# Where the streamed weight rows of a token-mixing kernel lie in SBUF

## The chip, the cores and the metric

The kernel runs on one core of one Trainium2 chip. The metric is device time in microseconds (us) of that core, as the median of several executions. TensorE (PE) does the matrix products, VectorE (DVE), ScalarE (ACT) and GpSimd (POOL) prepare operands and drain results, and SyncE (SP) issues the transfers.

SBUF, the memory from which all engines read, has 128 partitions. A tile occupies the same stretch of bytes in each partition. In this document a "word" is 4 bytes of one partition, and the "word of 64" of a row is its start address in words, modulo 64: a row that starts at byte 118,496 starts at word 29,624 and so at word 56 of 64.

## The reference

```
x  = causal 7-tap filter of x per head (softmax of `weight` as taps)     # 4 x 4224 x 192
theta = x @ w_theta
y  = w_tok_r @ (x * cos(theta)) + w_tok_i @ (x * sin(theta))             # w_tok: 4224 x 4224, twice
u  = x + y
x  = u + relu(u @ w_ch)
h  = U, V applied over the token axis (rank 32);  u = x + h
out = u + relu(u @ w_ch1) @ w_ch2                                         # 192 -> 768 -> 192
```

The two products with the 4224 x 4224 matrices `w_tok_r` and `w_tok_i` are most of the work. The weights arrive in 64-bit floating point. The kernel turns them into 32-bit values and splits each into an upper part (rounded for the matrix unit, type fp32r) and a lower part, the remainder.

## The kernel before

**Tokens and chunks.** The 4224 source tokens are 33 blocks of 128. The 4224 target tokens are nine chunks, `WIDE`: one of 480 columns, six of 464, two of 480. A step of `STEPS` is one chunk for two source blocks (a few steps at the start are two chunks for one block). For the last two source blocks the targets are eleven chunks of 384 (`LATE`).

**One group of matmuls.** `products` (L671) computes one output tile of 128 features by one chunk. For each of the two matrices (`q`) and each of the two source blocks (`k`) it issues three matmuls, L683: features' upper part by weights' upper row, upper by lower row, lower by upper row. That is 12 matmuls for a group, six groups for a step. The features (tile `z`) are the operand that is loaded into the array, 128 columns of it by a LDWEIGHTS ahead of each matmul. The weight row (tile `w`) is the operand that streams through. `evict` (L686) then adds the 128 x 464 or 128 x 480 sums into `yt` on DVE (L691).

**Where the rows lie.** The tile `w` (two buffers, pool `wp`, `weight_tile` at L607) has 8 x 480 words for each partition. `weight_part` (L595) cuts it: for the nine wide chunks the order is q, k, half, column, so an upper and a lower row of the same q and k stand 480 words apart, and 480 is 32 modulo 64. Half 0 is the lower row and half 1 the upper one. The eleven late chunks use another cut: all upper rows in the first half of the tile, all lower ones in the second, every row 448 words (7 x 64) after the last, from word 8 of the half on. The same tile serves after that for `w_ch1`, whose columns are then the loaded operand.

With the pools as they stand, both buffers of `w` begin at word 56 of 64. In the wide chunks lower rows are thus at word 56 and upper ones at word 24; late rows are all at word 0. The feature tiles `z` (pool `zp`, on the right-hand side) have all their blocks at word 24. Behind `wp` on the left lies `wraw`, the landing place of the raw weights. When it is given up, the tiles `hid`, `ot`, `vs` and `vt` of the last stage take its place, `hid` at word 40.

**The last stage.** For 22 pairs of batch and chunk, `up_mm` (L1158 to L1169) multiplies by `w_ch1` (five matmuls of 384 columns; the rows of `fq` at word 24 stream, blocks of `w` at word 8 are loaded) and `down` (L1200 to L1204) by `w_ch2` (five of 384; the rows of `hid` at word 40 stream, blocks of `cl` at word 24 are loaded).

**What sets the order.** The instruction order is written out by hand in tables (`OPENING`, `ENTRY`, `TURN`) and in between by the loop `mix`. While PE multiplies, ACT and DVE unpack and split the next weights (`split_w`), and the SP queue fetches the ones after that. None of the tables is touched.

Of the kernel before, what the change touches and what calls it, by code (L numbers as in the profile page):

```python
# [10 lines left out]
F32 = mybir.dt.float32  # L11
# [7 lines left out]
P = 128  # L19
# [12 lines left out]
COLS = 384  # L32
SPC = COLS // P
WIDTHS = [480] + [464] * 6 + [480] * 2
WIDE = [(sum(WIDTHS[:c]), w) for c, w in enumerate(WIDTHS)]
# [4 lines left out]
def mix_steps():  # L40

    def pairs(chunks, s):
        return [(s, 1, list(chunks[n : n + 2])) for n in range(0, len(chunks), 2)]

    steps = [(0, 1, [WIDE[0]])] + pairs(WIDE[1:EARLY], 0) + [(0, 2, [c]) for c in WIDE[EARLY:]]
    starts = [0, len(steps)]
    steps += [(1, 2, [c]) for c in WIDE[:EARLY]] + pairs(WIDE[EARLY:], 2)
    for s in range(3, NS, 2):  # L50
        starts.append(len(steps))
        steps += [(s, 2, [c]) for c in (WIDE if s < NS - 2 else LATE)]
    return steps, starts


EARLY = 5
STEPS, STARTS = mix_steps()


# [29 lines left out]
WSTEP = 480  # L89

LSTEP = 448
# [107 lines left out]
def mix_kernel(ctx, tc, xT, wcv, wth, wtok, wch, uu, vv, w1, w2, outT):  # L199
# [3 lines left out]
    def pool(name, bufs=1, side=None, space=None, stack=None):  # L203
        kw = dict(name=name, bufs=bufs, reuse_waits="tile")
        if side:
            kw["side"] = side
        if space is not None:
            kw["space"] = space
        return (stack or ctx).enter_context(tc.tile_pool(**kw))
# [52 lines left out]
    left = ExitStack()  # L262
# [2 lines left out]

    cst = pool("cst")
    yp = pool("yp")
    wp = pool("wp", bufs=2, stack=left)
    wrp = pool("wraw", bufs=2, stack=raw_st)

# [9 lines left out]
    with tc.manual_schedule():  # L280
# [314 lines left out]
        def weight_part(g, q, low):  # L595
            if g < n_chunks - len(LATE):
                kb, n, _ = pieces[2 * g]
                t = wt[g].rearrange("p (q k h n) -> p q k h n", q=2, k=2, h=2)
                return t[:, q, :kb, 1 - low, :n]
            t = wt[g][:, 4 * WSTEP * low : 4 * WSTEP * (low + 1)]  # L600
            if g < n_chunks:
                kb, n, _ = pieces[2 * g]
                t = t[:, 8 : 8 + 4 * LSTEP].rearrange("p (q k n) -> p q k n", q=2, k=2)
                return t[:, q, :kb, :n]
            return t[:, 2 * WSTEP * q + 16 : 2 * WSTEP * q + 16 + 2 * COLS]

        def weight_tile(g):  # L607
            if g not in wt:
# [2 lines left out]
        def split_w(g, q, part, eng=None):  # L611

            h = 2 * g + q
            if h >= len(pieces):
                return
            if part < 2:
                (unpack_parts, unpack_join)[part](raw[h])
                return
            if g > n_chunks:
                return  # L620
            weight_tile(g)
            hi, src = weight_part(g, q, 0), words(raw[h], 1, F32)
            if g < n_chunks:
                src = src.rearrange("p (k n) -> p k n", k=pieces[h][0])
            if part == 2:
                nc.scalar.copy(hi, src)  # L626
            else:
                eng = eng or (nc.gpsimd if g < STARTS[1] and h != 2 * OPENED + 3 else nc.vector)
                eng.tensor_tensor(out=weight_part(g, q, 1), in0=src, in1=f(hi), op=ALU.subtract)  # L629
                del raw[h]  # L630
                if h not in (2, 3):
                    load_w(h + 4 if h < 2 else h + 2)
# [38 lines left out]
        def products(g, j, r, q):  # L671
            s0, kb, ranges = STEPS[g]
            if q == 0:
                sums[g, j, r] = ps_mm.tile([P, WMAX], F32, name="acc", tag="acc")[:, : ranges[r][1]]
            ps = sums[g, j, r]
            n, last = q * kb * 3, kb * 6 - 1
            high, low = weight_part(g, q, 0), weight_part(g, q, 1)
            for i in range(kb):
                z = zt[s0 + i]
                zh = z[:, q, j * P : (j + 1) * P]  # L680
                zl = z[:, 2 + q, j * P : (j + 1) * P]
                for a, b in ((zh, high), (zh, low), (zl, high)):
                    mm(ps, a, b[:, i + r, :], start=n == 0, stop=n == last)  # L683
                    n += 1
# [409 lines left out]
        g = STARTS[-1]  # L1094
# [321 lines left out]
```

## Time and profile before

| | |
|---|---|
| median of 3 runs | 2964.04 us (2963.32 to 2964.55) |
| the profiled execution | 2963.67 us |
| its span, first to last instruction | 2961.9 us |
| PE busy in the span | 2948.1 us |
| DVE, ACT, POOL busy | 2495.3, 1554.3, 291.8 us |
| mean granted TensorE clock | 1.00 |
| matmuls at L683: of 464, 480 and 384 columns | 6696, 3348 and 792 |

A page of the profile gives busy times of the engines, a chain of work followed back from the last instruction, and groups of equal instructions. Matmuls overlap in the records (the duration of one is longer than the distance from its start to the next one's start), so what a matmul costs is read from starts: so many matmuls in so many microseconds of the chain, which lists PE's time without overlap.

### The profile page before, as it was taken

The page shows a single profiled execution, that of the slowest core. Times are in us where ns is not written, and L with a number is a line of the kernel's source. Part 1 is how long each engine was busy: PE and PEld are TensorE (multiplying, and loading weights), DVE is VectorE, ACT ScalarE, POOL GpSimd, SP SyncE. Part 2 cuts the span into 40 slices and gives each one's busy share as a digit, 9 for nine tenths or more (in the row PEclk, how much of TensorE's full clock was granted, in tenths as well). Part 3 has the DMA queues.
Part 4 walks back from the last instruction along what each step waited for, and adds up shares of the span by engine and source line. Part 5 has one row for each costly group of instructions (what it writes and reads, how often), then busy time and mean ns, then how long its engine had stood idle before and what let it go on. Part 6 is the DMA issues. An engine that isn't in the chain of part 4 may idle for free.

```text
span 2961.9 us, 39012 instructions
## 1 busy us (share of the span) xinstructions
PE 2948.1 (100%) x14994; PEld 2693.9 (91%) x14994; DVE 2495.3 (84%) x4133; ACT 1554.3 (52%) x2237; POOL 291.8 (10%) x254
## 2 busy tenths in 40 slices
PE   9999999999999999999999999999999999999999
PEld 8888888888888989898989898988889999999999
DVE  8799989888888888898989898989899897555555
ACT  7655545455555555554555554545456555444443
POOL 2110000010000000000000010100002002000000
PEclk9999999999999999999999999999999999999999
DMA  4443443443434434434334344343433221101110
GB/s 137 132 132 123 127 133 124 127 132 122 137 123 128 133 124 130 130 123 135 124 125 135 123 128 131 124 135 127 125 127 116 65 62 52 38 31 43 35 38 33
DMA packets 119002, 323.50 MB, mean 109 GB/s; under 512 B 6688, under 2 KB 40480, under 8 KB 118688
## 3 DMA queue, kind: packets, MB, share of 16 engines
q1 hardware_dynamic: 118416, 320.81, 33.6%
q8 instruction: 118, 1.93, 0.3%
q14 instruction: 68, 0.56, 0.1%
q10 hardware_dynamic: 400, 0.21, 0.0%
HBM read 308.01 MB, written 12.98 MB: 108 GB/s over the span
## 4 chain that ended last, share of the span: by engine, by line
PE 95%; DVE 4%; ACT 1%; issue 0%; DMA 0%; POOL 0%; DVEq 0%; POOLq 0%
PE acc L683 73%; PE ob L1201 2%; PE acc L1165 2%; PE acc L1169 2%; PE acc L1166 2%; PE oa L1202 2%; PE ob L1200 2%; PE oa L1204 2%; PE oa L1203 2%; PE acc L1167 2%; PE acc L1168 2%; PE pacc L912 1%; PE th L515 1%; PE th L516 1%; DVE yt L691 1%; PE th L518 1%
## 5 line engine op out<-in xcount | busy, mean ns | idle before, releaser
L683 PE MATMUL acc<-w,z 128*128 128x464 f32 (+2 forms) x10836 | 2287.3, 371 | 2.6 <-DVE yt L691 0.8
L683 PEld LDWEIGHTS acc<-w,z 128*128 128x128 f32 x10836 | 2018.7, 188 | 240.6 <-DVE yt L691 1.7
L691 DVE TENSOR_TENSOR yt<-acc,yt 128x464 f32<-128x464 f32 (+2 forms) x876 | 550.3, 634 | 213.3 <-PE acc L683 210.7
L626 ACT CAST w<-wraw 128x928 fp32r<-128x928 f32 (+3 forms) x291 | 303.5, 1043 | 635.1 <-DVE wraw L243 634.9
L238 DVE TENSOR_SCALAR wraw<-wraw 128x928 uint16<-128x928 uint16 (+4 forms) x305 | 368.8, 1210 | 11.8 <-ACT wraw L229 6.3
L629 DVE TENSOR_TENSOR w<-wraw,w 128x928 fp32r<-128x928 f32 (+2 forms) x282 | 365.0, 1294 | 0.0
L224 ACT ACTIVATE wraw<-wraw,consts 128x928 int32<-128x928 uint16 (+4 forms) x305 | 348.8, 1144 | 20.5 <-DMA wraw<-in_wtok 15.8
L243 DVE SCALAR_TENSOR_TENSOR wraw<-wraw 128x928 int32<-128x928 int32 (+4 forms) x305 | 342.0, 1121 | 10.1
L229 ACT ACTIVATE wraw<-wraw 128x928 f32<-128x928 f32 (+3 forms) x296 | 310.2, 1048 | 3.7 <-DMA wraw<-in_wtok 2.9
L577 POOL TENSOR_TENSOR z<-tz,z 128x384 fp32r<-128x384 f32 x121 | 125.2, 1034 | 1706.3 <-ACT z L574 1706.3
L452 DVE SCALAR_TENSOR_TENSOR xa<-xr,tap,xa 128x256 f32<-128x256 f32 x744 | 285.6, 425 | 0.0
L1177 DVE SCALAR_TENSOR_TENSOR hid<-acc,hid 128x384 fp32r<-128x384 f32 x264 | 146.9, 557 | 149.3 <-ACT hid L1174 148.3
L1174 ACT ACTIVATE hid<-acc 128x384 fp32r<-128x384 f32 x264 | 129.8, 492 | 250.2 <-PE acc L1169 233.8
L574 ACT CAST z<-tz 128x384 fp32r<-128x384 f32 x129 | 66.2, 513 | 289.4 <-DVE tz L563 289.3
L583 POOL TENSOR_TENSOR yt<-yt,xa 128x384 f32<-128x384 f32 x64 | 70.2, 1097 | 248.6 <-DVE xa L452 195.4
L1201 PE MATMUL ob<-hid,cl 128*128 128x384 f32 x264 | 89.2, 338 | 0.1
L1165 PE MATMUL acc<-fq,w 128*128 128x384 f32 x264 | 89.2, 338 | 0.0
L1169 PE MATMUL acc<-fq,w 128*128 128x384 f32 x264 | 89.0, 337 | 0.0
L1202 PE MATMUL oa<-hid,cl 128*128 128x384 f32 x264 | 88.8, 336 | 0.0
L1204 PE MATMUL oa<-hid,cl 128*128 128x384 f32 x264 | 88.8, 336 | 0.0
L1203 PE MATMUL oa<-hid,cl 128*128 128x384 f32 x264 | 88.8, 336 | 0.0
L1200 PE MATMUL ob<-hid,cl 128*128 128x384 f32 x264 | 88.7, 336 | 0.0
(239 smaller groups left out, 2655.2 us busy)
## 6 DMA issues: line engine op xcount, KB each, us to landing
wraw<-in_wtok SPq DMA_DIRECT2D x184, 928.0 KB, 4.7
wraw<-in_wtok SPq DMA_DIRECT2D x92, 960.0 KB, 4.9
wraw<-in_wtok SPq DMA_DIRECT2D x22, 768.0 KB, 4.4
xr<-in_xT SPq DMA_DIRECT2D x63, 201.0 KB, 2.6
outT<-ot SPq DMA_DIRECT2D x20, 576.0 KB, 3.0
vzw<-in_vv SPq DMA_DIRECT2D x10, 384.0 KB, 4.1
wraw<-in_w SPq DMA_DIRECT2D x3, 768.0 KB, 4.3
yt<-in_wtok SPq DMA_DIRECT2D x2, 928.0 KB, 8.8
```

The costliest lines, as they stand in the source:

```text
L224: nc.scalar.activation(words(raw, 0), words(raw, 1, U16), AF.Identity, scale=2.0**-13, bias=consts[:, 3:4])
L229: nc.scalar.activation(w, w, AF.Copy, scale=2.0**-112)
L238: nc.vector.tensor_scalar(out=words(raw, 1, U16), in0=words(raw, 3, U16), scalar1=0x8000, scalar2=None, op0=ALU.bitwise_and)
L243: nc.vector.scalar_tensor_tensor(out=words(raw, 1), in0=words(raw, 1), scalar=3, in1=words(raw, 0), op0=ALU.logical_shift_left, op1=ALU.bi ...
L452: nc.vector.scalar_tensor_tensor(out=xa, in0=src, scalar=w, in1=xa, op0=ALU.mult, op1=ALU.add)
L626: nc.scalar.copy(hi, src)
L629: eng.tensor_tensor(out=weight_part(g, q, 1), in0=src, in1=f(hi), op=ALU.subtract)
L683: mm(ps, a, b[:, i + r, :], start=n == 0, stop=n == last)
L691: nc.vector.tensor_tensor(out=dst, in0=ps, in1=dst, op=ALU.add)
L1165: mm(ps, w[0], q[:, b, :], start=True, stop=False)
L1169: mm(ps, w[3], q[:, 4 + b, :], start=False, stop=True)
L1201: mm(ob, c2[:, m, 2, :], h[:, 1, :], start=False, stop=last)
```

## The change

Three things are altered, none of which adds, removes or moves an instruction: each engine's list is the same as before, operation by operation and with the same waits.

- A pool `gap` of 16 words is allocated ahead of `wp`. All that lies behind it on the left moves by 16 words: `w` begins at word 8 of 64, `wraw` too, `hid` moves from word 40 to 56, and `ot`, `vs`, `vt` likewise.
- A table `ROWS` gives each wide chunk a pair (turn, skip). `turn` exchanges the places of the upper and the lower row, `skip` starts both rows 0, 8 or 16 words later inside their 480 words.
- The constants for the late chunks and for `w_ch1` are adjusted: late rows come to word 40 (from 0), `w_ch1` stays at word 8.

Upper / lower row, word of 64:

| chunk | columns | before | after |
|---|---|---|---|
| 0, 7 | 480 | 24 / 56 | 40 / 8 |
| 8 | 480 | 24 / 56 | 8 / 40 |
| 1 | 464 | 24 / 56 | 40 / 8 |
| 2 | 464 | 24 / 56 | 48 / 16 |
| 3 | 464 | 24 / 56 | 56 / 24 |
| 4 | 464 | 24 / 56 | 8 / 40 |
| 5 | 464 | 24 / 56 | 16 / 48 |
| 6 | 464 | 24 / 56 | 24 / 56 |
| late | 384 | 0 / 0 | 40 / 40 |

The features `z` stay at word 24.

```diff
@@
 EARLY = 5
+ROWS = {
+    o: r
+    for (o, _), r in zip(WIDE, [(0, 0), (0, 0), (0, 8), (0, 16), (1, 0), (1, 8), (1, 16), (0, 0), (1, 0)], strict=True)
+}
@@
     yp = pool("yp")
+    pool("gap", stack=left).tile([P, 16], F32, name="gap")
     wp = pool("wp", bufs=2, stack=left)
@@
                 t = wt[g].rearrange("p (q k h n) -> p q k h n", q=2, k=2, h=2)
-                return t[:, q, :kb, 1 - low, :n]
+                _, _, ((o, _), *_) = STEPS[g]
+                turn, skip = ROWS[o]
+                return t[:, q, :kb, 1 - low ^ turn, skip : skip + n]
             t = wt[g][:, 4 * WSTEP * low : 4 * WSTEP * (low + 1)]
             if g < n_chunks:
                 kb, n, _ = pieces[2 * g]
-                t = t[:, 8 : 8 + 4 * LSTEP].rearrange("p (q k n) -> p q k n", q=2, k=2)
+                t = t[:, 32 : 32 + 4 * LSTEP].rearrange("p (q k n) -> p q k n", q=2, k=2)
                 return t[:, q, :kb, :n]
-            return t[:, 2 * WSTEP * q + 16 : 2 * WSTEP * q + 16 + 2 * COLS]
+            return t[:, 2 * WSTEP * q : 2 * WSTEP * q + 2 * COLS]
```

## Rows read from the trace of the kernel before

**Rows 1.** The page, busy time of each engine, share of the span, instructions
```profile
span 2961.9 us, 39012 instructions
...
PE 2948.1 (100%) x14994; PEld 2693.9 (91%) x14994; DVE 2495.3 (84%) x4133; ACT 1554.3 (52%) x2237; POOL 291.8 (10%) x254
...
PEclk9999999999999999999999999999999999999999
```

**Rows 2.** The page, the chain that ended last, by engine and by line
```profile
PE 95%; DVE 4%; ACT 1%; issue 0%; DMA 0%; POOL 0%; DVEq 0%; POOLq 0%
```

**Rows 3.** Groups by shape: count, busy us, mean ns of one, idle before
```profile
L683 PE MATMUL acc<-w,z 128*128 128x464 f32 x6696 | 1411.5, 371 | 0.9 <-DVE yt L691 0.8
L683 PE MATMUL acc<-w,z 128*128 128x480 f32 x3348 | 731.7, 379 | 1.0 <-POOL z L577 0.7 <-ACT z L574 0.2
...
L683 PE MATMUL acc<-w,z 128*128 128x384 f32 x792 | 149.8, 340 | 0.7 <-DVE yt L880 0.7
```

**Rows 4.** Who waited for whom: us in total, times, longest
```profile
DVE yt L691 <- PE acc L683: 210.7, 229, 2.7
...
ACT wraw L224 <- DMA wraw<-in_wtok: 15.8, 25, 1.9
```

**Rows 5.** The chain, wide chunks, 1200 to 1420 us: start, us, what
```profile
1208.79 46.73 PE acc L683 x216
...
1256.77 30.11 PE acc L683 x144
...
1288.13 30.11 PE acc L683 x144
...
1319.49 30.20 PE acc L683 x144
...
1350.93 46.73 PE acc L683 x216
```

**Rows 6.** The chain, late chunks of 384 columns, 2290 to 2430 us
```profile
2297.15 9.38 PE acc L683 x54
2310.01 2.12 PE acc L683 x12
2313.13 2.09 PE acc L683 x12
...
2421.37 2.12 PE acc L683 x12
```

**Rows 7.** PE's instructions in order, last stage: start, us, line, shape
```profile
2563.78 0.34 PE L1200 MATMUL ob<-hid,cl 128*128 128x384 f32 x1
...
2564.65 0.34 PE L1165 MATMUL acc<-fq,w 128*128 128x384 f32 x1
...
2565.51 0.34 PE L1200 MATMUL ob<-hid,cl 128*128 128x384 f32 x1
```

**Rows 8.** DMA issues: size of each, median us from issue to landing
```profile
wraw<-in_wtok SPq DMA_DIRECT2D x184, 928.0 KB, 4.7
```

## The prediction

> **What bounds the kernel now.** I read the engines' busy times first. PE is busy for 2948.1 of 2961.9 us and the granted clock is in its top tenth in all forty slices, which is the 2.4 GHz level throughout [rows 1]. The chain that ended last says the same in another way: 95% of it is PE [rows 2]. The groups by shape say what on PE: L683 has 6696 matmuls of 464 columns, 3348 of 480 and 792 of 384, and PE stood idle ahead of the whole of them for 0.9, 1.0 and 0.7 us [rows 3]. So nothing that feeds or drains these matmuls is late. DVE waits 210.7 us in all for L683's sums [rows 4], which means that DVE is ahead of PE, and a raw weight tile lands 4.7 us after its issue [rows 8] while ACT waits for such transfers for 15.8 us in all [rows 4]. The time of this kernel is therefore a number of matmuls times the distance from the start of one to the start of the next, and only a change of that distance can change it much.
>
> **The distances.** In the chain, 216 matmuls of 480 columns take 46.73 us, 216.3 ns each, and 144 of 464 take 30.11 us, 209.1 ns each; one stretch of 144 takes 30.20 [rows 5]. As a yardstick I take one column for each cycle of 2.4 GHz: 200.0 and 193.3 ns. What is above that, the excess, is 16.3 ns for a 480 row and 15.8 ns for a 464 row. In the last stage ten matmuls of 384 columns, five of L1200 to L1204 and five of L1165 to L1169, take 2565.51 - 2563.78 = 1.73 us, 173.0 ns each [rows 7], and the yardstick is 160.0: an excess of 13.0 ns. The late chunks, also 384 columns, run in two manners: 54 matmuls in 9.38 us, 173.7 ns each, an excess of 13.7, or twelve in 2.12 us, 176.7 ns each, an excess of 16.7, beside groups of twelve at 2.09 [rows 6]. The stretch holds 14 groups at 2.12 and one more follows, so 15 x 12 = 180 matmuls.
>
> What differs between these? The same engine, the same clock, the same type of operand. The streams of the last stage start 16 words (modulo 64) from the block that is loaded beside them (24 against 8, 40 against 24); late rows start at 0 with features at 24; the wide chunks stream rows at 24 and at 56 with features at 24, that is 0 and 32 words away. And two groups of the same late chunk, with equal addresses, differ by 3 ns a matmul [rows 6]. So there is some state that holds over a group, and the excess lies between 13.0 and 16.7 ns. The wide rows, at 15.8 and 16.3, stand in the upper half of this interval.
>
> **The change part by part.** It adds no instruction and moves none. It alters the places of streamed rows, and each part is priced by the bounds 13.0 and 16.7 ns, the best and the worst that long stretches show. Nothing in the trace shows a wide row anywhere but at 24 and 56, so for a row that comes to a new place I take the middle of the bounds, 14.9 ns (from 16.3 a gain of 1.4, from 15.8 one of 0.9), and keep both ends.
>
> The three chunks of 480 columns go to 40 and 8, 16 words on either side of the features. 3348 matmuls x -1.4 ns = -4.7 us; at the ends -3.3 ns, -11.0 us, and +0.4 ns, +1.3 us.
>
> Four chunks of 464 columns (1, 2, 4, 5) go to new words. Each of the six has 6696 / 6 = 1116 matmuls, so 4464 x -0.9 ns = -4.0 us; ends -2.8 ns, -12.5 us, and +0.9 ns, +4.0 us. Chunk 6 ends where it was, at 24 / 56: nothing. Chunk 3 has the same two words with upper and lower exchanged, so that two of three matmuls now stand 32 words away instead of one; I take nothing, ends -3.1 and +1.0 us.
>
> The late rows go from 0 to 40, which is the distance of 16 words that the last stage has. I take the slow manner as gone: 180 matmuls x (176.7 - 173.7) = -0.5 us; ends -0.5 and, if all 792 fell into the slow manner, 612 x 3.0 = +1.8 us.
>
> `hid` moves from word 40 to 56, from 16 to 32 words away from `cl`. There are 264 matmuls on each of the five lines L1200 to L1204, 1320 in all, now at the lower bound: they can only lose by these rows. Middle: 1320 x 1.9 ns = +2.5 us; ends 0 and 3.7 ns, +4.9 us.
>
> Other engines: the unpacking and splitting on ACT and DVE read and write the same tiles 16 words further on. If one of their instructions grew by some per cent it would eat into 210.7 us in which DVE waits for PE [rows 4]; it would show only if that cover went, and each 1% of DVE's 2495.3 us [rows 1] is 25 us, so some 8% could go before. The transfers land at other offsets; they have a whole step, 72 matmuls x 0.21 = 15 us for two transfers, against 4.7 us each [rows 8]. Both at nothing.
>
> Sum: -4.7 - 4.0 - 0.5 + 2.5 = -6.7 us. From the profiled execution's 2963.67 us that is 2957.0; the median of the runs is 0.4 us above the profiled one, so 2957.4 us. All lower ends: -11.0 - 12.5 - 3.1 - 0.5 = -27.1, 2937. All upper ends: 1.3 + 4.0 + 1.0 + 1.8 + 4.9 = +13.0, 2977.
>
> **The rivals.** The first: the words do not matter, and the excess depends on the row's width and on whether a row begins where the last one ended. The widths fit: 384 columns 13.0 to 13.7, 464 columns 15.8, 480 columns 16.3 [rows 5 to 7]. Both rows of a pair still stand 32 words apart, so all steps from row to row stay as they were. Against it speaks the late chunk with its two manners at one width [rows 6]. It gives no more than the late chunks' 0.5 us: 2963.5 us. The Trainium skill has two rules that end here. "TensorE: Matmul & The Clock Gate" (Step-by-step: what each phase is for) says that the streamed and the loaded operand come through two independent SBUF read ports and that loading does not take bandwidth from the running matmul; by that no word relative to the features could count. "SBUF — State Buffer" (Specifications (TRN2)) gives lines of 16 bytes, each crossing of which costs; all words here, old and new, are multiples of four words, so the number of lines in a row would stay the same. By both the sum is 0. What the first page gives for back-to-back matmuls, columns over 2.4 plus 2.5 ns, would be 195.8 ns for 464 columns by that page's figure, and the trace's 209.1 does not agree: some 13 ns of each matmul are not in that account, which is why I do not let the rule decide.
>
> The second rival ends slower. The state that makes late rows slow can be one that new places make usual, and then worse than the trace shows: one further loss of the size seen between the late manners, 3.0 ns, for each matmul of the seven wide chunks that really move. Price: 7812 x 3.0 = +23 us if all seven fall, 2987 us; some +12 us, 2976 us, if half do. It decides from a quarter on: 5.9 us (0.2%) / 3.0 ns = 1970 of 7812 matmuls. For it: the only rows at a multiple of 16 words, the late ones, are the only ones seen slow at 384 columns, and chunks 2 and 5 go to 48 and 16. Against it: late rows at the same word also run at 173.7.
>
> A third: the gain goes all the way. Rows 16 words from the features ran at the lower bound in the last stage; if that distance is what counts, the 480 chunks and chunks 1 and 4 come down to 13.0 ns: -11.0 and 2232 x -2.8 = -6.2 us, in all about -17 us, 2947 us. For it speaks the constancy of 173 ns over the last stage, against it that width is mixed with distance in every row I have.
>
> **How the numbers follow.** Some gain, from the middle to the whole of it (2940 to 2958): 0.40, and the middle, 2957.4, is the forecast. No change: 0.35. Slower, by the second rival: 0.25. About 0.2%, 5.9 us, is what a measurement of this kernel can tell from no change. So faster 0.40, same 0.35, slower 0.25. For 8 in 10 the range takes the third case but not all lower ends, and the second with half of the matmuls: 2942 to 2977. As cases of both signs hold much of the chance, the forecast's own range stands apart: 2942 to 2962.
>
> **What would show it.** The instruction groups keep their counts, and PE's idle time ahead of L683 stays near 1 us. The chain's long runs decide: 216 matmuls of 480 columns in less than 46.73 us (46.4 at the middle, 46.0 at the lower bound), and runs of 144 at 464 that differ from chunk to chunk, with those of chunks 3 and 6 near 30.1. If all runs stay at 30.1 and 46.7 the first rival has it. If some run reads over 30.6 or 47.4, the second has. Late groups of twelve should all read 2.08 to 2.09. Ten matmuls of the last stage at more than 1.73 us are `hid`'s doing. The forecast is wrong if the six chunks of 464 show six different excesses whose mean is not below 15.8, for then the present place was simply a good one.

## The result, and the profile after

The changed kernel takes 2983.18 us (median of three runs, 2982.80 to 2983.42) against 2964.04: a ratio of 1.0063 with a 95% interval of 1.0050 to 1.0077. It is slower by 19.1 us, where 2957.4 was forecast, and lies above the range of 2942 to 2977.

The page of the kernel after, busy time of each engine and the granted clock:

```profile
span 2981.6 us, 39012 instructions
...
PE 2967.7 (100%) x14994; PEld 2694.4 (90%) x14994; DVE 2497.2 (84%) x4133; ACT 1552.6 (52%) x2237; POOL 291.2 (10%) x254
...
PEclk9999999999999999999999999999999999999999
```

The span grew by 19.7 us and PE's busy time by 19.6 [rows 1]. The other engines' times moved by 2 us at most, and the clock stayed at the 2.4 GHz level. The groups by shape (count, busy us, mean ns of one, idle before) and the wait of DVE for PE, of the kernel after, in which the old L683 is L693 and L691 is L701:

```profile
L693 PE MATMUL acc<-w,z 128*128 128x464 f32 x6696 | 1424.0, 373 | 0.6 <-DVE yt L701 0.6
L693 PE MATMUL acc<-w,z 128*128 128x480 f32 x3348 | 737.9, 381 | 1.0 <-POOL z L585 0.8 <-ACT z L582 0.2
...
L693 PE MATMUL acc<-w,z 128*128 128x384 f32 x792 | 148.5, 338 | 0.8 <-DVE yt L890 0.8
```

```profile
DVE yt L701 <- PE acc L693: 225.7, 229, 2.8
```

The counts are those of [rows 3] and PE's idle time is still about 1 us, so no wait was added: 12.5 us went into the 464 rows, 6.2 into the 480 rows, and 1.3 came back from the late ones. DVE waits 15 us longer for PE [rows 4]: it is PE that became slower, and DVE has more time than before.

The chain of the kernel after, 1200 to 1420 us (start, us, what). The runs of 216 are chunks 7, 8 and 0, the three runs of 144 are chunks 1 and 2, 3 and 4, 5 and 6:

```profile
1218.16 47.16 PE acc L693 x216
...
1266.57 30.65 PE acc L693 x144
...
1298.46 30.15 PE acc L693 x144
...
1329.86 30.40 PE acc L693 x144
...
1361.50 47.16 PE acc L693 x216
```

Against [rows 5] the 480 chunks lost 0.43 us for 216 matmuls, chunks 1 and 2 0.54 us for 144, chunks 5 and 6 some 0.25, chunks 3 and 4 next to nothing. Asked for stretches inside single steps, the same chain gives one row for each place. In order: 480 columns at 40/8 and 8/40 (upper/lower row), then chunks 1 to 6 at 40/8, 48/16, 56/24, 8/40, 16/48 and 24/56:

```profile
1504.84 10.91 PE acc L693 x50
...
1519.91 11.66 PE acc L693 x53
...
1553.25 10.68 PE acc L693 x50
...
1567.95 11.31 PE acc L693 x53
...
1585.14 10.47 PE acc L693 x50
...
1599.59 11.07 PE acc L693 x53
...
1616.54 10.63 PE acc L693 x50
...
1631.17 11.07 PE acc L693 x53
```

Divided by the number of matmuls, that is 218.2 and 220.0 ns at 480 columns, and at 464 columns 213.6, 213.4, 209.4, 208.9, 212.6 and 208.9. Chunks 1 and 4 have the same two words with upper and lower row exchanged: chunk 1 (40/8) loses, chunk 4 (8/40) does not.

The late chunks in the chain, and PE's instructions in the last stage (start, us, line, shape) of the kernel after:

```profile
2315.15 9.36 PE acc L693 x54
...
2327.96 2.08 PE acc L693 x12
2331.04 2.08 PE acc L693 x12
```

```profile
2583.41 0.33 PE L1210 MATMUL ob<-hid,cl 128*128 128x384 f32 x1
...
2584.29 0.34 PE L1175 MATMUL acc<-fq,w 128*128 128x384 f32 x1
...
2585.16 0.33 PE L1210 MATMUL ob<-hid,cl 128*128 128x384 f32 x1
```

The groups at 2.12 of [rows 6] are gone, and ten matmuls of the last stage take 1.75 us against 1.73 [rows 7].

From the starts of all matmuls of a class in the two traces, the whole of it adds up:

| class | matmuls | ns before | ns after | us |
|---|---|---|---|---|
| 480, chunks 0 and 7 | 2232 | 216.7 | 217.9 | +2.6 |
| 480, chunk 8 | 1116 | 216.7 | 220.0 | +3.7 |
| 464, chunk 1 | 1116 | 209.1 | 213.4 | +4.8 |
| 464, chunk 2 | 1116 | 209.1 | 213.0 | +4.3 |
| 464, chunk 5 | 1116 | 209.1 | 212.4 | +3.7 |
| 464, chunks 3, 4, 6 | 3348 | 209.1 | 209.3, 209.0, 209.0 | -0.1 |
| late | 792 | 174.8 | 173.2 | -1.3 |
| last stage, from its first start to its last | 2640 | 471.0 us | 473.4 us | +2.4 |
| sum | | | | +20.1 |

The mean of the six 464 chunks rose from 209.1 to 211.0 ns. So where the time came from is no question. The question is what makes a place good or bad.

### The profile page after: what moved, and what is told of

The parts are those of the page before. It is cut to its first block, busy times and chain, and to the rows that moved or that the text cites. A ratio compares the mean times of both kernels' runs of the same rounds, so it can differ in the third digit from the quotient of the medians.

```text
span 2981.6 us, 39012 instructions
## 1 busy us (share of the span) xinstructions
PE 2967.7 (100%) x14994; PEld 2694.4 (90%) x14994; DVE 2497.2 (84%) x4133; ACT 1552.6 (52%) x2237; POOL 291.2 (10%) x254
## 4 chain that ended last, share of the span: by engine, by line
PE 94%; DVE 4%; ACT 1%; DMA 1%; issue 0%; POOL 0%; DVEq 0%; POOLq 0%; ACTq 0%; SPq 0%
PE acc L693 73%; PE acc L1175 2%; PE oa L1213 2%; PE oa L1212 2%; PE ob L1211 2%; PE acc L1176 2%; PE oa L1214 2%; PE ob L1210 2%; PE acc L1177 2%; PE acc L1178 2%; PE acc L1179 2%; PE th L523 1%; PE th L524 1%; PE th L526 1%; DVE wraw L245 1%; PE pacc L922 1%
## 5 line engine op out<-in xcount | busy, mean ns | idle before, releaser
L693 PE MATMUL acc<-w,z 128*128 128x464 f32 (+2 forms) x10836 | 2304.7, 373 | 2.4 <-DVE yt L890 0.8
L693 PEld LDWEIGHTS acc<-w,z 128*128 128x128 f32 x10836 | 2017.4, 188 | 258.9 <-DVE yt L701 1.4
L701 DVE TENSOR_TENSOR yt<-acc,yt 128x464 f32<-128x464 f32 (+2 forms) x876 | 551.0, 635 | 228.3 <-PE acc L693 225.7
```

Source lines behind the costliest of these rows:

```text
L701: nc.vector.tensor_tensor(out=dst, in0=ps, in1=dst, op=ALU.add)
```

## The experiments

**The theories.** By the first, what counts is how far the streamed rows stand from the feature block that is loaded between them. I write such a distance as upper/lower row minus block, modulo 64 words: before, every wide chunk has 0/32; after, chunk 1 has 16/48, chunk 2 24/56, chunk 3 32/0, chunk 4 48/16, chunk 5 56/24, chunk 6 0/32. By the second, a row's own word counts, whatever the features' place, be it by itself or by a conflict with what writes to `w`. The two part as soon as the features are moved.

**The features moved under the same rows.** In the kernel after, `z` goes from word 24 to word 40.

```diff
-    pool("room", side="right", stack=right).tile([P, 32], F32, name="room")
+    pool("room", side="right", stack=right).tile([P, 16], F32, name="room")
```

> The changed kernel with the features z moved 16 words too (word 24 to 40; the padding on the right-hand side is 16 words shorter). Streamed rows stay where the changed kernel has them. Theory 1, only the distance between streamed row and loaded block counts: chunk 1 (now 0 and 32 words away) reads 208.9 ns a matmul as in the kernel before, chunk 4 (32 and 0) 209.3 as chunk 3 has after the change, chunk 6 (48 and 16) 209.0, chunk 3 (16 and 48) 213.4; chunks 0 and 7 of 480 (0 and 32) 216.7. Theory 2, only the streamed row's own word counts: all chunks keep the times of the changed kernel, chunk 1 213.4, 2 213.0, 3 209.3, 4 209.0, 5 212.4, 6 209.0, chunks 0 and 7 217.9, chunk 8 220.0 ns, and the whole stays at 2983 us within 3 us.

2974.15 us against 2963.68 for the kernel before, ratio 1.0035 (1.0021 to 1.0048): by the ratios 0.0063 - 0.0035 = 0.0028, some 8 us of the loss, went, though no weight row was touched. The chain of this kernel inside single steps (L693 is the old L683): 480 columns at rows 8/40, then chunks 1, 3 and 4.

```profile
1512.43 11.44 PE acc L693 x53
...
1545.39 10.47 PE acc L693 x50
...
1576.94 10.68 PE acc L693 x50
...
1591.62 11.07 PE acc L693 x53
```

The 480 row at 8/40, 220.0 ns after, is at 11.44 / 53 = 215.8, with its distance at 32/0. Chunk 1 at 40/8, the worst after, is now at 10.47, as fast as 0/32 was before, and 0/32 is its new distance. Chunk 3 at 56/24, good after, now stands at 16/48 and has taken over chunk 1's 10.68. Over all starts the six chunks read 209.5 (0/32), 211.1 (8/40), 213.1 (16/48), 208.9 (32/0), 210.5 (40/8) and 209.1 (48/16); the four distances that both kernels have agree within 0.6 ns. For the 464 columns the row's own word is refuted as the cause. By the starts the wide chunks gave back 11.3 us; the move took back 1.7 of them elsewhere, as the late rows came to distance 0 (174.1 ns) and the rows of `fq` to 32 words from `w_ch1`.

**Single parts undone and done alone.**

```diff
-            fo.tile([P, 112], F32, name="room", tag="room")
+            fo.tile([P, 96], F32, name="room", tag="room")
```

> The changed kernel with hid, ot, vs and vt back at word 40 (a padding 16 words shorter ahead of them). If the place of hid costs what the two traces' last stage shows, ten matmuls go back to 1.733 us and the whole falls by 2 us, to 2981 us. If the last stage's loss came from elsewhere, it stays at 2983 us. The wide chunks keep their times in both.

2980.57 us, ratio 1.0059 (1.0045 to 1.0072). That is 2.6 us under the kernel after by the medians and 1.2 by the ratios, which the times alone can't tell from nothing. The trace can: the last stage is back at 471.1 us by its starts, from 473.4. In PE's instructions of this kernel, ten matmuls are back at 1.73 us:

```profile
2582.06 0.34 PE L1210 MATMUL ob<-hid,cl 128*128 128x384 f32 x1
...
2582.93 0.34 PE L1175 MATMUL acc<-fq,w 128*128 128x384 f32 x1
...
2583.79 0.34 PE L1210 MATMUL ob<-hid,cl 128*128 128x384 f32 x1
```

```diff
-    for (o, _), r in zip(WIDE, [(0, 0), (0, 0), (0, 8), (0, 16), (1, 0), (1, 8), (1, 16), (0, 0), (1, 0)], strict=True)
+    for (o, _), r in zip(WIDE, [(0, 0)] + [(1, 16)] * 6 + [(0, 0)] * 2, strict=True)
```

> The changed kernel with the rows of all six chunks of 464 back at 24 / 56; the 480 and late chunks and hid as the change has them. If each chunk's loss is its own, the six chunks read 208.9 to 209.1 ns, 13 us are gone and 2970 us are left, of which 6 us above the kernel before are the 480 chunks and 2 us hid, less 1 us of the late chunks. If the loss hangs on changing places from chunk to chunk, the 480 chunks also return to 216.7 ns and the whole comes to 2964.

2969.12 us, ratio 1.0018 (1.0009 to 1.0027). The six chunks of 464 are back at 209.1 ns. The new table does one thing more than its expectation says: it also turns chunk 8 from 8/40 to 40/8, where it reads 217.8 instead of 220.0 ns, 2.4 us less. So the 1.0063 - 1.0018 = 0.0045, 13 us, are not the 464 chunks alone; by the starts these are 12.7 us, 15.1 with chunk 8, which agrees with 13 within the intervals of the two ratios. What stays is the 480 chunks, now all at 16/48 (217.9 ns, +3.8 us), `hid` and the late rows. That chunks 0 and 7 kept their 217.9 ns shows that their loss does not come from the places of the 464 chunks. The chain of this kernel, a stretch of 480 and one of 464:

```profile
1510.98 11.55 PE acc L693 x53
...
1544.15 10.47 PE acc L693 x50
```

In the kernel before, the late rows alone, from word 0 to 40:

```diff
-                t = t[:, 8 : 8 + 4 * LSTEP].rearrange("p (q k n) -> p q k n", q=2, k=2)
+                t = t[:, 48 : 48 + 4 * LSTEP].rearrange("p (q k n) -> p q k n", q=2, k=2)
```

> The kernel before with the late rows alone moved from word 0 to word 40. If 16 words from the features is a good place for a row of 384, the late groups of twelve all read 2.08 to 2.09 us and the whole is 1 us shorter, 2963 us. If the late chunks' two manners come from what precedes them (transposes, waits) and not from the place, groups of 2.12 us stay and the time is 2964 us.

2962.68 us against 2963.68, ratio 0.9998 (0.9989 to 1.0007). The trace shows the gain: late matmuls at 173.3 ns in the mean instead of 174.8, 1.2 us over all 792, and no group of twelve at 2.12. The times can't tell it from nothing. The late groups in the chain of this kernel:

```profile
2296.13 9.36 PE acc L683 x54
...
2308.94 2.08 PE acc L683 x12
```

**A map of distances.** In the kernel before, a table gives each wide chunk the offsets of its upper and lower row freely. The features stay at 24. All four kernels have the 480 chunks at 32/0, and the late rows at 40.

```diff
+PLACES = {o: p for (o, _), p in zip(WIDE, [(0, 480), (464, 0), (0, 464), (496, 32), (32, 496), (480, 16), (16, 480), (0, 480), (0, 480)], strict=True)}
...
-                t = wt[g].rearrange("p (q k h n) -> p q k h n", q=2, k=2, h=2)
-                return t[:, q, :kb, 1 - low, :n]
+                _, _, ((o, _), *_) = STEPS[g]
+                t = wt[g].rearrange("p (q k m) -> p q k m", q=2, k=2)
+                at_word = PLACES[o][low]
+                return t[:, q, :kb, at_word : at_word + n]
```

> The kernel before with new places for its wide rows, given as distance of the upper and of the lower row from the features, modulo 64 words: chunks 1 to 6 at 48/32, 32/48, 16/0, 0/16, 0/48, 48/0; the three 480 chunks at 32/0; late rows at 16. The distance theory, from runs so far: the 480 chunks read 216.0 ns (the value chunk 8 had at 32/0), 2.5 us less than before, the late groups 2.08 us. For the six chunks: if a row's excess depends on its own distance alone, 16/0 and 0/16 come down to the 206.7 ns that rows of 384 at 0 and 16 suggest (excess 13.3); if the pair of distances or the step between the two rows counts, they read 209 to 213 like all pairs so far, and no pair says anything on another.

2971.92 us, ratio 1.0028 (1.0018 to 1.0039). Two exchanges of the same two rows, in the chain of this kernel (the old L683 is L686 here): 48/32 and 32/48, then 16/0 and 0/16:

```profile
1546.20 10.47 PE acc L686 x50
...
1560.67 11.25 PE acc L686 x53
...
1577.82 10.57 PE acc L686 x50
...
1592.39 11.07 PE acc L686 x53
```

Which of the two rows streams twice in three matmuls matters: 209.3 against 212.3 ns, and 211.1 against 209.0, over all starts. 480 columns at 32/0 run at 215.8, better than before.

The other three have other pairs in the same table:

```diff
+... zip(WIDE, [(0, 480), (496, 0), (0, 496), (8, 472), (472, 8), (488, 24), (24, 488), (0, 480), (0, 480)], strict=True)}
```

> As the run before, with chunks 1 to 6 at distances 16/32, 32/16, 40/56, 56/40, 8/56, 56/8 (upper / lower); 480 chunks at 32/0, late rows at 16. Own distance alone: 16/32 and 32/16 read below 209 ns, as rows at 16 were fast in the last stage, and the pairs around 40 and 56 read 212 to 213, as pairs with 24 and 56 did. Pair or step counts: an exchange of upper and lower changes a chunk by more than 2 ns in at least one of the three couples, as 16/48 against 48/16 did (213.4 and 209.0).

```diff
+... zip(WIDE, [(0, 480), (480, 0), (484, 4), (4, 484), (492, 12), (12, 492), (16, 496), (0, 480), (0, 480)], strict=True)}
```

> As the run before, with chunks 1 to 6 at distances 0/32, 4/36, 36/4, 12/44, 44/12, 48/16; 480 chunks at 32/0, late rows at 16. Chunk 1 reads 208.9 ns and chunk 6 209.0, as both distances have read so far. If the distance acts in steps of 8 or 16 words, 4/36 reads as 0/32 (208.9) and 12/44 as 8/40 (211.1); if every word counts, they lie in between or elsewhere, up to 213.4.

```diff
+... zip(WIDE, [(0, 480), (496, 4), (496, 8), (492, 0), (488, 0), (28, 492), (20, 496), (0, 480), (0, 480)], strict=True)}
```

> As the other maps of pairs: chunks 1 to 6 at distances 16/36, 16/40, 12/32, 8/32, 60/12, 52/16; 480 chunks at 32/0, late rows at 16. If 16/32, which held 207.8 ns in three groups of four and 210.9 in the others, marks a good neighbourhood, one of 16/36, 12/32 and 8/32 holds 207.8 ns or less throughout, and six chunks of that would save 9 us. If it does not, all six read 208.9 to 213.4 like the eighteen pairs so far, and no place of the 464 rows beats the one before by more than 0.2 ns.

They took 2970.51, 2964.36 and 2968.03 us (one run each). Mean distance from start to start at 464 columns, from all starts of the class, of these four kernels and of the kernel after:

| ns | distances upper/lower |
|---|---|
| 208.9 to 209.5 | 0/32, 32/0, 48/16, 0/16, 16/32, 48/32, 4/36, 44/12, 60/12 |
| 210.0 to 210.8 | 32/16, 12/32, 8/32, 36/4, 16/36, 52/16, 0/48 |
| 211.1 to 211.6 | 16/0, 16/40, 40/56, 56/40, 8/56, 56/8 |
| 212.2 to 213.5 | 32/48, 56/24, 12/44, 24/56, 48/0, 16/48 |

In the second kernel neither expectation came out: no exchange changed more than 1.2 ns (16/32 against 32/16), where over 2 was expected, and the four pairs with 40 or 56 read 211.2 to 211.5 instead of 212 to 213. In the third, 4/36 reads as 0/32, but 36/4 lies 1.0 ns above 32/0 and 12/44 lies 1.4 above the 8/40 of the kernel with the features moved, so the distance does not act in steps of 8 or 16 words.

No place tried is better than 208.9: the place of before was already a good one for 464 columns. In the second kernel 56 groups of 12 at 16/32 held 207.8 ns and 20 others about 211, so I looked around that pair with the last kernel; four words beside it (12/32, 16/36) it is 210.0 and 210.6, and that hope fell.

**Only one row.** Does each row cost by its own distance, so that a pair is a mean, two parts of the upper row to one of the lower? In this kernel the second of the three matmuls streams the upper row too.

```diff
-            high, low = weight_part(g, q, 0), weight_part(g, q, 1)
+            high, low = weight_part(g, q, 0), weight_part(g, q, 0 if g < n_chunks - len(LATE) else 1)
```

> The kernel before with late rows at 40, in which the second matmul of each triple streams the upper row again instead of the lower one (the product with the lower row is left out), so that all rows that stream in a chunk stand at one distance: 0, 16, 32, 48, 40, 56 for chunks 1 to 6, 32 for the 480 ones. If the excess is a matter of the mixing of two distances, 464 columns at one distance come down to what 384 columns have at one distance: 206.7 ns at 0 and 16 (excess 13.3), up to 210.0 at 40. If the width counts beside the distance, 0 and 16 stay near 209 ns. For each distance it also says what a row at that distance costs by itself: if pairs are means of their two distances, 48/16 must be two parts of 48 and one of 16.

2991.26 us (one run). The chain of this kernel, 464 columns at the single distances 0, 16, 32 and 48:

```profile
1559.50 10.51 PE acc L686 x50
...
1574.01 11.13 PE acc L686 x53
...
1591.04 10.69 PE acc L686 x50
...
1605.78 11.31 PE acc L686 x53
```

Its late rows, 384 columns at the single distance 16:

```profile
2324.40 9.36 PE acc L686 x54
...
2337.21 2.08 PE acc L686 x12
```

At 464 columns that is 210.2, 210.0, 213.8 and 213.4 ns; over all starts 210.0, 210.0, 213.5 and 213.3, and 212.4 and 211.3 at 40 and 56. By a mean of 210 and 213.5, 0/32 would come to 211.2 and 48/16 to 212.3; both measured 209.1. And 16/0 and 0/16 read 211.1 and 209.0, though 0 and 16 alone read the same. The pair has a price of its own, and going from one place to another can be better than staying.

Two questions were settled beside it. Late rows, 384 columns at distance 16, run at 173.3 ns, an excess of 13.3 over columns / 2.4; 464 columns at the same distance 16 have 210.0 - 193.3 = 16.7. So the excess is not one number for all widths: it is 8.3% of columns / 2.4 in the one case and 8.6% in the other, about in proportion to the columns. And 480 columns at distance 32 take 219.9, so 220 ns is not peculiar to chunk 8 of the kernel after; the excess there is 9.9%, and 10.4% for 464 columns at 32.

**Everything moved together.** First the features alone in the kernel before (same change as in the first experiment, no weight row touched), which brings all wide chunks to 48/16, the late rows to 24 and the rows of `fq` to 32:

> The kernel before with all streamed weight rows where they were (24 / 56, late 0) and only the features and the other tiles of the right-hand side moved by 16 words (z from word 24 to 40). If the distance counts, all wide chunks now stand at 48/16: the 464 chunks read 209.0 ns as chunk 4 did after the change, and the 480 chunks 220.0 as chunk 8 did, although no weight row moved: 3348 x 3.3 ns = 11 us, and 3 us more in the last stage, where the rows of fq come 32 words from their blocks: 2978 us. If the rows' own words count, the chunks keep 209.1 and 216.7 ns and the time is 2964 us.

2967.38 us against 2964.05, ratio 1.0011 (1.0002 to 1.0021). The chain of this kernel, a stretch of 480 and one of 464, and a late group:

```profile
1507.95 11.48 PE acc L683 x53
...
1540.96 10.47 PE acc L683 x50
```

```profile
2310.07 2.12 PE acc L683 x12
```

464 columns came out as in the map, 209.1. The late rows all fell into the slow manner, 176.6. The last stage lost 3.4 us: in the up product (by `w_ch1`), whose streams now stand 32 words from their blocks, a matmul lost 3.4 ns, and in `down`, now at distance 0, it gained 0.7. But 480 columns read 216.7 ns, where the same distance 48/16 had given 220.0 in chunk 8 of the kernel after. That was a miss, and it asked whether distance is enough. So rows by 32 words and features by 16, both, with late rows at distance 16 and `w_ch1` at word 8 by their own constants (not shown):

```diff
+PLACES = {o: p for (o, _), p in zip(WIDE, [(0, 480), (0, 480), (480, 0), (8, 488), (488, 8), (16, 496), (496, 16), (0, 480), (0, 480)], strict=True)}
...
+    pool("gap", stack=left).tile([P, 32], F32, name="gap")
...
-    pool("room", side="right", stack=right).tile([P, 32], F32, name="room")
+    pool("room", side="right", stack=right).tile([P, 16], F32, name="room")
```

> Weight tiles 32 words further on than in the kernel before and features 16 (z at 40): the three 480 chunks at 48/16 by words 24/56 with the upper row first of its pair; chunks 1 to 6 at 48/16, 16/48, 56/24, 24/56, 0/32, 32/0 (upper / lower), late rows at 16; in the last stage both streams 32 words from their blocks. For 480 columns at 48/16 two values are known, 220.0 ns (words 8/40, upper row first) and 216.7 (words 24/56, lower row first). If the order of the two rows in the tile, 480 words up or down, makes the difference, the 480 chunks read 220.0; if the rows' own words count beside the distance, 216.7. The 464 chunks by the distance: 209.0, 213.4, 212.4, 213.0, 209.0, 209.1 ns; a chunk that differs by more than 0.5 ns from its value shows that the distance alone doesn't settle it there either.

2985.56 us (one run; the kernel before 2962.90 beside it). At 464 columns the distances foretold all six chunks: 209.4 (48/16), 213.1 (16/48), 212.4 (56/24), 213.1 (24/56), 209.3 (0/32), 209.1 (32/0), each within 0.5 ns of the same distance elsewhere. The last stage took 479.3 us by its starts, 8.3 more, with both of its streams 32 words from their blocks: 176.6 ns a matmul of 384 columns, an excess of 10.4% where 464 columns at the single distance 32 have 10.4 too. The 480 chunks showed what had been missed. The chain of this kernel (the old L683 is L687), ahead of and behind the products of theta (L517 to L521) that break into a step of 480 columns, and a later stretch without them:

```profile
1497.14 2.85 PE acc L687 x13
```

```profile
1499.99 0.15 PE th L517
...
1501.15 0.09 PE th L521
1501.24 33.83 PE acc L687 x156
```

```profile
1516.22 11.48 PE acc L687 x53
```

Thirteen matmuls ahead of theta, twelve of them of 480 columns, take 219 ns each; behind it 53 take 216.6, with rows and features at the same addresses. By the starts of the whole trace, a group of 480 that follows directly on a 464 chunk at 32/0 ran 48 cycles of 2.4 GHz a matmul over its columns (220 ns), and so did those behind it until theta came: 15 times of 15, 18 groups of twelve in all. Of the others 236 held 40 (216.7 ns), and the 16 right behind theta begin with one matmul of some 246 ns and go over to 40 within themselves. So one pair of places can run in two manners at the same addresses, and a break by other products ended the slower one each time.

That the chunk ahead brings it on fits two more traces, but isn't shown by them. In the kernel with the features alone, where the chunk ahead is at 48/16, the groups that follow it directly read 39, but its upper row lies behind the lower one in the tile. In the kernel after, chunk 8 always follows on a 480 chunk at 16/48, and all its 90 groups read 48, but its rows and features stand at other words. No run changed the chunk ahead alone.

**The best places put together.** 480 columns at 32/0, 464 at 48/16, late rows at 40, features where they were (rows cut by the table as in the map):

```diff
+PLACES = {o: p for (o, _), p in zip(WIDE, [(0, 480), (16, 496), (16, 496), (16, 496), (16, 496), (16, 496), (16, 496), (0, 480), (0, 480)], strict=True)}
...
-                t = t[:, 8 : 8 + 4 * LSTEP].rearrange("p (q k n) -> p q k n", q=2, k=2)
+                t = t[:, 48 : 48 + 4 * LSTEP].rearrange("p (q k n) -> p q k n", q=2, k=2)
```

> The kernel before with the places that read best so far: the three 480 chunks at distances 32/0 (215.85 ns against 216.74 before), the six 464 chunks at 48/16 (208.97 against 209.13), late rows at 16 (0.8 us), hid at word 40 as before. If each class's spacing is set by its own distances and nothing else, the sum is 3348 x -0.89 ns - 6696 x 0.16 ns - 0.8 us = -4.9 us, 2959 us. If a chunk's excess also hangs on the chunk before it, the runs of 144 matmuls differ from 30.1 us and the gain is not kept.

2958.59 us (11 runs, 2958.03 to 2959.91) against 2963.33: ratio 0.9984 (0.9975 to 0.9993), faster than both kernels. The chain of this kernel, a stretch of 480 and one of 464:

```profile
1505.05 11.42 PE acc L686 x53
...
1537.90 10.47 PE acc L686 x50
```

480 columns run at 215.8 ns, 3348 x 0.9 = 3.0 us less than before, the late rows give about 1.3, and 464 columns give next to nothing; the medians differ by 4.7 us.

## Why the prediction was wrong, step by step

**What bounds the kernel** held: no idle time was added, DVE's wait for PE grew from 210.7 to 225.7, and the whole change is in the distances from start to start.

**The bounds are the step that failed.** The excess was taken to lie between 13.0 and 16.7 ns for every width, "the best and the worst that long stretches show", with the middle for any new place. But both ends came from rows of 384 columns, and the one-row kernel showed that the excess goes with the width: the same distance 16 costs 13.3 ns at 384 columns and 16.7 at 464. Read as a share of columns / 2.4, the rows of the kernel before said so already: 13.0 of 160.0 is 8.1% and 16.7 is 10.4%, while the wide rows had 15.8 of 193.3 and 16.3 of 200.0, 8.2% both [rows 5 to 7]. By these shares the bounds are 15.7 to 20.2 ns at 464 columns and 16.3 to 20.9 at 480, and the wide rows stood at the lower end, not "in the upper half". All runs together reached 15.5 to 20.2 ns at 464 columns and 15.8 to 20.0 at 480 as means of a class. The middle that was taken, 14.9, is under anything that a whole class of wide rows reached, so the change had almost nothing to win on them and some 4 ns a matmul to lose. The last sign of being wrong that the prediction names came true: the mean excess of the six chunks of 464 is 17.7, not below 15.8, and the present place was simply a good one.

**The terms.** 480 chunks: -4.7 us forecast, upper end +1.3, measured +6.3. 464 chunks 1, 2, 4, 5: -4.0, upper end +4.0, measured 4.8 + 4.3 - 0.1 + 3.7 = +12.7. Chunk 3: 0, measured +0.2. That was luck: it was set to nothing without a reason, and other exchanges of the same two rows cost up to 4.4 ns a matmul. Late rows: -0.5, measured -1.3 in the kernel after and -1.2 alone. The manner that was to go was right, its count too small: by the mean of 174.8 about half of the 792 late matmuls ran slowly before, and not only the 180 in groups of twelve. `hid`: +2.5, measured +2.4 by the starts, and gone when it was undone. Late rows and `hid` are priced from rows of their own width. The two large ones were missed by 11.0 and 16.7 us, and that is all of the miss of 26 us and a little more.

**The rivals.** The second gave 12 to 23 us and came nearest: six of the seven chunks that move lost, 2.4 ns a matmul over all seven, against its 3.0. What it had for itself was not right: it suspected words that are a multiple of 16, while chunk 1 at 40/8 lost most of the 464 chunks, chunk 4 at 8/40 lost nothing, and moving the features exchanges such roles. Its sign, a run of 144 over 30.6 us, was there (30.65), and its full price, 2987 us, covers the result; the range stopped at half of it. The third named the right quantity, the distance, and the wrong value: 16 words is good for the late rows and is the worst for a wide upper row whose lower row stands at 48. The first, that words don't matter, is refuted by chunks 1 to 6, though its other half, that the excess goes with the width, is borne out.

The Trainium skill's "TensorE: Matmul & The Clock Gate" (Step-by-step: what each phase is for) has two independent SBUF read ports for the streamed and the loaded operand, by which a distance between them could not count; the traces do not agree, with 209.1 and 213.4 ns for the same instruction at 0/32 and 16/48. It was right not to let it set the sum.

**What stays open.** Shown is that moving rows or features by a few words changes the spacing, that at 464 columns the distance between them foretells it, and that one pair of addresses can run in two manners. Through what part of the chip is not: the features could be moved only together with everything that lies behind them on the right-hand side, and no record of the trace shows PE's reads. That 64 words are the period is taken and not tested. Nor is it tested whether the number of columns acts by itself or by the word at which a row ends, since the two go together in every run. The table of distances is measured, not explained, and for 480 columns only 32/0, 0/32, 16/48, 48/16 and 32 alone were tried.

## What to carry to other kernels

Where one engine is busy for the whole span and each of its instructions runs a fixed distance behind the last, that distance is itself a quantity to be measured by place, and the present place says nothing about the others: a price from one place is no upper bound, and one from another width has to be taken per column before it is compared. Find good places by giving every chunk of one kernel a different place and reading each chunk's spacing from a single trace, then put the best together and time that, as was done here in a few such traces for 4.7 us. Place the streamed rows relative to the block that is loaded, not absolutely, and expect any change of a pool ahead of either to move all of it.

## What the runs showed of the hardware

- Matmuls of fp32r with a load ahead of each took from 207.8 ns (groups at 16/32) to 213.5 ns at 464 columns, 215.8 to 220.0 at 480 and 173.0 to 176.7 at 384, at the 2.4 GHz level throughout. Taken modulo 64 words, the distance between streamed rows and loaded block decided most of it: at 464 columns, six distances measured again under other absolute words came out within 0.6 ns.
- What such a matmul took over columns / 2.4 grew about in proportion to the columns: at the single distance 16 it was 8.3% (384 columns) and 8.6% (464), at 32 it was 10.4, 10.4 and 9.9% (384, 464 and 480).
- Exchanging the two rows of a pair changed the spacing by up to 4.4 ns (48/16 against 16/48), and two rows at two distances can be faster than one row alone (0/32 at 209.1, single distances 0 and 32 at 210.0 and 213.5).
- The same addresses can run in two manners: late rows at distance 40 at 173.7 and 176.7 ns [rows 6], 480 columns at 48/16 at 216.7 and 220.0. In the kernel with rows and features both moved, each of 15 entries from a 464 chunk at 32/0 took the slower one, and the next break by other products ended it.
